# A chunked linear-attention and adapter kernel: 15 of 24 key products move from VectorE to GpSimd, gate selection moves to VectorE, and the written order is replaced

## The chip, the cores and the metric

The kernel runs on one core of a Trainium2 chip. The metric is device time in microseconds (us), from several executions of the whole kernel; lower is better. One execution was taken with the hardware profiler. Its page gives a span, from the first to the last instruction, and the run itself a slightly longer time.

The engines are TensorE (PE, with weight loads as PEld), VectorE (DVE), ScalarE (ACT), GpSimd (POOL) and SyncE (SP), which here only issues transfers. Each works through its own queue in order.

## The reference

Shapes are batch 4, 8 heads, 768 steps, head width 48. An attention with a decaying state is followed by a mixture of 8 adapters of rank 16, of which each row uses 2.

```python
for t in range(S):                                   # per batch and head
    cur = einsum('bhd,bhe->bhde', u[None] * kt, vt)
    y[:, :, t] = einsum('bhd,bhde->bhe', rt, state + cur)
    state = wt[:, :, :, None] * state + einsum('bhd,bhe->bhde', kt, vt)
...
x = y.transpose(0, 2, 1, 3).reshape(B * S, H * D)    # 3072 x 384
logits = x @ w_gate                                  # 8 adapters
topk = the 2 largest of each row;  w = exp(sel) / (sum + 1e-9)
out = x + sum over the 2 adapters e of  w * ((x @ A[e]) @ B[e])
```

## The kernel before

The rows are cut into 24 tiles of 128 steps. Tiles 0 to 5 are the chunks of the first batch, 6 to 11 of the second, and so on. Eight heads of 48 channels are kept as four pairs (`P` = 4), each pair on 128 partitions with the 48 channels of a head padded to 64. Logarithms of the decay are summed along a chunk by matrix products, so that within a tile the recurrence becomes two products with exponentials, a masked 128 x 128 score matrix per head, and a state that is carried from tile to tile.

The steps of one tile, by their names in the order string, with the engine that does them:

- `load_rk`, `load_w` (two tiles at once), `store`: transfers on SP's queue. `load_v`: a transfer on POOL's queue, which turns float32 into float16; `VGROUPS` says how many tiles each one brings. `rk_in` has 12 buffers, `w_in` 8, `res` 16.
- `ln` (ACT): logarithm of two tiles of decay. `cs` (PE): cumulative sums into the one buffer `cs_ps`. `expP`, `expN` (ACT): exponentials of the sum and of its negative, into `eP` and `eN`, one PSUM buffer each.
- `multR`, `multK` (DVE, lines 264 and 268): r times `eP` and k times `eN`, called `rseq` and `kT` in the profile.
- `kT` (PE, line 317): four transposes of the k product. `kev`: their copy to SBUF. `kv` (PE): the state's update in PSUM. `sev`: the state's copy to SBUF.
- `amm` (PE, line 305): scores. `aev` (DVE, line 311): scores times the mask. 
- `rku` (POOL, line 278): r times k, `dg` (PE): its sums with u, `dgev` (ACT): their copy for two tiles, `dv` (POOL, line 295): v times those sums.
- `yd`, `yA` (PE): the output y in PSUM. `yev`: its copy `xT`.
- `lg` (PE), `gate` (ACT, the exponential), `gmax` (DVE: largest values, sum, reciprocal), `gsel` (POOL, lines 393 to 396: which of the 8 values reach the second largest, times their weight), `z` (PE), `zw` (DVE), `zT` (PE), `zTev`: the adapters, in `BATCHES` of 4, 4, 4, 4, 4, 3 and 1 tiles; a step's number is that of the last tile of its batch.
- `d` (PE), `oev`: result and its copy `res`, which `store` writes out.

The order of all of this is written out by hand in the string `PLAN`, some 616 tokens such as `multK.7`. Walking through it issues each step's instructions, and every engine runs its own in that order. The copies go through one helper, which picks ACT or DVE; a star after a token swaps the two. The PSUM tiles `y_ps`, `kn_ps`, `z_ps`, `zT_ps`, `d_ps` and the warming `j_ps` come from one ring of two buffers. `setup` fills constants and runs `JUNK` warming matrix products.

```python
    for f, t, other in plan():
        side["other"] = other
        fns[f](t)
```

The functions that the change touches:

Of the kernel before, what the change touches and what calls it, by code (L numbers as in the profile page):

```python
# [8 lines left out]
F32 = mybir.dt.float32  # L9
# [12 lines left out]
VGROUPS = {0: 1, 1: 3, 4: 4, 8: 4, 12: 4, 16: 4, 20: 4}  # L22
JUNK = 8

PLAN = """
    setup.0 load_wa.0 load_w.2 load_wb.0 ln.0 cs.0 ln1.0 expN.0 expP.0 load_rk.0 load_rk.1 ln.2 junk.13 junk.3 cs.1
    multK.0 kT.0 multR.0 amm.0 kev.0 expN.1 junk.5 adapters.0 load_w.4 expP.1 multK.1 multR.1 cs.2 aev.0 casts.0*
    kT.1 load_rk.2 expN.2 multK.2 load_v.0 load_v.1 rku.1 junk.2 kv.0 expP.2 rku.0 dg.0 dg.1 cs.3 multR.2 load_rk.3
    amm.1 kev.1* dgev.1 ln.4 load_rk.4 sev.0 aev.1 load_w.6 dv.0 load_rk.5 yd.0 expP.3 load_rk.6 expN.3 kv.1
    load_v.4 sev.1 multR.3 yA.0 kT.2 multK.3 rku.2 cs.4 rku.3 yev.0 kev.2 amm.2 expP.4 dv.1 load_w.8 dg.2 rku.4 kT.3  # L30
    load_rk.7 expN.4 multR.4 dg.3 cs.5 multK.4 ln.6 yd.1 dgev.3 aev.2 rku.5 kv.2 dv.2 yA.1 expP.5 expN.5 dg.4
    multK.5 yev.1 kev.3* cs.6 multR.5 sev.2 dv.3 load_rk.8 amm.3 kT.4 dg.5 expN.6 kv.3 expP.6 yd.2 kev.4* rku.6 yA.2
    load_w.10 sev.3 cs.7 lg.1 aev.3 multK.6 yev.2 amm.4 yd.3 dgev.5 multR.6 dg.6 expN.7 expP.7 ln.8 yA.3 kT.6 kev.6*
    yev.3 load_w.12 aev.4 kv.4 lg.0 amm.5 dv.4 sev.4 multK.7 cs.8 multR.7 yd.4 kT.7 lg.2 rku.7 dg.7 expP.8 dv.5
    load_v.8 load_rk.9 lg.3 expN.8 adapterB.0 dgev.7 aev.5 kev.7* yA.4 multR.8 load_rk.10 amm.6 multK.8 kv.6
    load_rk.11 dv.6 rku.8 cs.9 yev.4 ln.10 gate.3 load_w.14 expP.9 expN.9 aev.6 yd.5 rku.9 yd.6 yA.5 amm.7 yev.5
    gmax.3 multR.9 yA.6 aev.7 multK.9 cs.10 yev.6 kT.8 gsel.3 z.3 sev.6 lg.5 dv.7 load_rk.13 ln.12 amm.8 kv.7 kev.8*
    kT.9 expP.10 zw.3 dg.9 dg.8 expN.10 yd.7 rku.10 load_rk.12 load_rk.14 dgev.9 kev.9* aev.8 load_rk.15 multR.10
    dv.8 load_w.16 yA.7 rku.11 sev.7 cs.11 zT.3 kv.8 multK.10 load_w.18 yev.7 zTev.3 dv.9 castB.0 dg.10 amm.9
    expP.11 sev.8* kT.10 d.0 kev.10 dg.11 load_v.12 expN.11 multR.11 rku.13 multK.11 cs.12 rku.12 ln.14 oev.0  # L40
    expP.12 d.1 oev.1 lg.4 expN.12 aev.9 yd.8 lg.7 kv.9 dgev.11 multR.12 yA.8 dv.10 yd.9 cs.13 amm.10 dv.11 sev.9
    yev.8 yA.9 expP.13 rku.14 multK.12 kv.10 d.2 dg.12 expN.13 aev.10 yev.9 rku.15 lg.6 cs.14 multR.13 gate.7 yd.10
    multK.13 oev.2 yA.10 store.0 sev.10 expP.14 amm.11 kT.12 dg.13 load_rk.16 lg.8 yev.10 expN.14 gmax.7 lg.9 kev.12
    kT.13 gsel.7 store.2 dgev.13 d.3 kev.13* oev.3 ln.16 aev.11 multR.14 cs.15 multK.14 z.7 kv.12 zw.7 expP.15 dv.13
    dv.12 ln.18 rku.16 amm.12 dg.14 kT.14 expN.15 dg.15 yd.11 yA.11 dgev.15 store.1 load_v.16 lg.10 load_rk.18 cs.16
    load_rk.17 kev.14* dv.15 yev.11 sev.12 zT.7 yd.12 aev.12 amm.13 yA.12 multR.15 store.3 rku.18 multK.15 expP.16
    zTev.7 expN.16 kv.13 aev.13 lg.11 multR.16 yev.12 dg.16 load_rk.19 gate.11 multK.16 d.7 oev.7 cs.17 d.4 sev.13
    yd.13 oev.4 gmax.11 amm.14 store.7 kv.14 yA.13 d.5 store.4 expP.17 expN.17 dv.14 aev.14 multR.17 yev.13 multK.17
    dg.18 lg.12 cs.18 kT.16 oev.5 rku.17 dg.17 kev.16* amm.15 kT.15 z.11 sev.14 kev.15* expP.18 yd.14 expN.18 yA.14
    aev.15 gsel.11 kv.15 zw.11 amm.16 rku.19 store.5 lg.13 load_w.20 load_rk.22 yev.14 zT.11 d.6 multK.18 cs.19  # L50
    dgev.17 zTev.11 sev.15 load_rk.21 oev.6 expN.19 d.9 yd.15 aev.16 store.6 oev.9 yA.15 amm.17 multR.18 aev.17
    dg.19 lg.14 d.8 yev.15 store.9 expP.19 oev.8 multR.19 dv.16 load_rk.20 ln.20 yd.16 lg.15 yA.16 kv.16 amm.18
    kT.18 load_rk.23 yev.16 gate.15 multK.19 kev.18 dv.17 rku.22 dgev.19 cs.20 sev.16 load_w.22 kT.19 gmax.15
    expP.20 store.8 load_v.20 kev.19 rku.21 d.10 oev.10 kv.18 dg.22 expN.20 dv.18 yd.17 sev.18 store.10 aev.18
    rku.20 yd.18 yA.17 yA.18 gsel.15 kv.19 amm.19 yev.17 yev.18 cs.21 dg.20 multK.20 kT.20 multR.20 aev.19 z.15
    expN.21 dv.19 lg.18 kev.20* multK.21 d.11 expP.21 dg.21 rku.23 amm.20 zw.15 lg.16 kT.21 ln.22 lg.17 oev.11 dg.23
    kev.21* sev.19 dgev.21 cs.22 zT.15 yd.19 yA.19 dgev.23 dv.20 expN.22 aev.20 multR.21 kv.20 zTev.15 multK.22
    yev.19 amm.21 d.12 yd.20 sev.20 dv.21 aev.21 oev.12 yA.20 yd.21 yA.21 kv.21 expP.22 lg.19 yev.20 d.13 multR.22
    yev.21 amm.22 sev.21 gate.19 dv.22 store.11 kT.22 cs.23 oev.13* d.15 kev.22* gmax.19 gsel.19 oev.15 store.12
    z.19 store.13 expP.23 yd.22 aev.22 zw.19 yA.22 kv.22 expN.23 multR.23 lg.21 yev.22 zT.19 d.14 zTev.19 sev.22  # L60
    multK.23 lg.20 lg.22 oev.14 d.16 gate.22 d.18 amm.23 gmax.22 oev.16 aev.23 oev.18 dv.23 d.17 store.15 gsel.22
    oev.17 z.22 zw.22 store.14 yd.23 yA.23 store.16 zT.22 yev.23 lg.23 zTev.22 d.21 d.19 gate.23 store.18 gmax.23
    oev.21 store.17 oev.19 d.22 z.23 oev.22 gsel.23 zw.23 store.21 zT.23 d.20 zTev.23 store.19 oev.20 d.23 store.22
    oev.23 store.20 junk.12 store.23
# [20 lines left out]
def kernel(  # L85
# [10 lines left out]
    NT, L = rk.shape[0], 128  # L96
# [42 lines left out]
    def load_rk(t):  # L139
        rk_in = io.tile([L, 2, P, NQ], F32, name="rk_in", bufs=12)  # L140
        nc.sync.dma_start(out=rk_in, in_=rk[t])
        st[t]["rk"] = rk_in
# [8 lines left out]
    w_sb = const.tile([128, P, ER + E + 2], F32, name="w_sb")  # L151
    w16 = const.tile([128, P, ER + E + 2], FP16, name="w16")
# [98 lines left out]

    def expN(t):
        nc.scalar.activation(out=eN, in_=cs_ps, func=ACT.Exp, scale=-1.0)  # L253

    def mult_half(t, q):
        c = t % NC
        if c == 0 and q == 0:
            r_ = wk.tile([128, P, NC * 128 + 1], BF16, name="rseq")
            nc.vector.memset(r_[:, :, 0:1], 0.0)
            for i in range(NC):  # L260
                st[t + i]["rseq"] = r_
        a = c * 128
        if q == 0:
            nc.vector.tensor_mul(st[t]["rseq"][:, :, a + 1:a + 129], st[t]["rk"][:, 0, :, 1:129], eP)  # L264
            st[t]["rT"] = st[t]["rseq"][:, :, a:a + 128]
        else:
            st[t]["kT"] = wk.tile([128, P, 128], BF16, name="kT", bufs=3)
            nc.vector.tensor_mul(st[t]["kT"], st[t]["rk"][:, 1, :, 1:129], eN)  # L268
# [7 lines left out]
    def rku(t):  # L276
        p_ = wk.tile([128, P, 128], FP16, name="rku", bufs=3)
        nc.gpsimd.tensor_mul(p_, st[t]["rk"][:, 0, :, 0:128], st[t]["rk"][:, 1, :, 1:129])  # L278
        st[t]["rku"] = p_
# [34 lines left out]
    def kT(t):  # L314
        kn_ps = ring([128, H, 64], BF16, "kn_ps")
        for p in range(P):
            nc.tensor.transpose(kn_ps[:, 2 * p:2 * p + 2].rearrange("s a d -> s (a d)"), st[t]["kT"][:, p, :], ident)  # L317
        st[t]["kn_ps"] = kn_ps
# [22 lines left out]
    def yd(t):  # L341
# [5 lines left out]
        if t % NC > 0:  # L347
            for p in range(P):
                nc.tensor.matmul(y_ps[:, p, :], lhsT=st[t - 1]["S"][:, p].rearrange("a g e -> a (g e)"),  # L349
                                 rhs=s_["rT"][:, p], start=False, stop=False, skip_group_check=True)  # L350
# [11 lines left out]
    def yev(t):  # L362
        xT = wk.tile([128, P, 128], FP16, name="xT", bufs=10)
        copy("ACT", xT, st[t]["y_ps"])
        st[t]["xT"] = xT

    def lg(t):
        for p in range(P):
            nc.tensor.matmul(lg_ps[:, t % NSLOT, :], lhsT=st[t]["xT"][:, p, :], rhs=w16[:, p, ER:ER + E],
# [9 lines left out]
    def gmax(t):  # L379
# [4 lines left out]
        for i in range(n):  # L384
            nc.vector.max(out=top[:, i, :], in_=ge[:, i, :])
        nc.vector.tensor_reduce(out=den, in_=top[:, :, 0:2], axis=AX.X, op=ALU.add)
# [3 lines left out]
    def gsel(t):  # L390
        t0, n = gate_at[t]
        g = wk.tile([L, GMAX, E], F32, name="g")[:, 0:n, :]
        nc.gpsimd.tensor_sub(g, st[t]["ge"], st[t]["top"][:, :, 1:2].to_broadcast([L, n, E]))
# [3 lines left out]
        st[t]["g"] = g  # L397

    def z(t):
        t0, n = gate_at[t]  # L400
        z_ps = ring([L, GMAX, ER], F32, "z_ps")
        for i in range(n):
            for p in range(P):
                nc.tensor.matmul(z_ps[:, i, :], lhsT=st[t0 + i]["xT"][:, p, :],
# [3 lines left out]
    def zw(t):  # L408
        t0, n = gate_at[t]
        zw_ = wk.tile([L, GMAX, E, R], FP16, name="zw")  # L410
        nc.vector.tensor_mul(
# [3 lines left out]
        st[t]["zw"] = zw_  # L415
# [95 lines left out]
```

## Time and profile before

| | |
|---|---|
| median of 3 runs | 93.3 us (92.87 to 94.39) |
| profiled execution, its own time | 94.24 us |
| its span | 92.5 us |
| busy: PE / DVE / ACT / POOL | 78.5 / 71.8 / 73.2 / 57.4 us |
| busy share of the DMA engines by the loads and stores on SP's queue | 66.2% of the span |
| the same by the v loads on POOL's queue | 14.3% |

In the rows of instruction groups "mean ns" is one instruction from start to end. Instructions of one engine overlap a little, so that counts times means come to more than the busy time: for DVE the groups add up to some 79 us against 71.8 busy, for ACT to some 88 against 73.2. Idle time stands with what ended it, inferred from semaphores. PE's busy time is modelled and a busy PE is not necessarily PE at its peak.

### The profile page before, as it was taken

Reading aid. Unit: us, or ns where it says so; the run is one execution under the profiler, and the core shown is the slowest. Engines: PE = TensorE matmul, PEld = TensorE weight load, DVE = VectorE, ACT = ScalarE, POOL = GpSimd, SP = SyncE. Lnnn points to the kernel's source line nnn. Section 1 sums busy time; section 2 is a strip of 40 time slices with the busy share of each in tenths; the row PEclk is TensorE's granted clock in tenths of the full one; section 3 lists DMA queues with packets and bytes.
Section 4 is the critical chain, followed back from the end, with each engine's and each line's share of the span. In section 5 each row is a group of like instructions: output and inputs, shape, how many; then the busy total and the mean of one; then the engine's idle time right before and its main releaser. Section 6 shows DMA issues by size and latency. Waiting matters only on the chain.

```text
span 92.5 us, 3554 instructions
## 1 busy us (share of the span) xinstructions
PE 78.5 (85%) x1430; PEld 61.2 (66%) x1430; DVE 71.8 (78%) x150; ACT 73.2 (79%) x163; POOL 57.4 (62%) x95
## 2 busy tenths in 40 slices
PE   2964855699899999799999999999959799998760
PEld 1323543585778888598888879887757578966420
DVE  5205918986989999998999999999499587987310
ACT  5219593988899999999999999899753997884640
POOL 6700939905996984999989984539378181612300
PEclk9999999957999999999999999999999999999999
DMA  1989999999999999999989997999995102418163
GB/s 34 262 296 328 283 409 416 378 292 403 416 417 401 394 284 377 413 360 257 311 227 352 293 215 223 348 355 327 278 250 155 64 32 92 170 43 301 46 252 137
DMA packets 10097, 25.19 MB, mean 272 GB/s; under 512 B 1120, under 2 KB 4704, under 8 KB 10080
## 3 DMA queue, kind: packets, MB, share of 16 engines
q1 hardware_dynamic: 9072, 22.60, 66.2%
q0 software_dynamic: 1008, 2.36, 14.3%
q8 instruction: 11, 0.18, 0.8%
q14 instruction: 6, 0.05, 0.2%
HBM read 22.60 MB, written 4.72 MB: 295 GB/s over the span
## 4 chain that ended last, share of the span: by engine, by line
DMA 43%; PE 22%; DVE 15%; POOL 6%; issue 4%; ACT 3%; SPq 3%; POOLq 0%; DVEq 0%
DMA rk_in<-in_rk_dram 21%; DMA w_in<-in_w_dram 10%; DMA v<-in_v_dram 9%; DVE at L311 7%; POOL rku L278 4%; DVE rseq L264 3%; PE y_ps L359 3%; PE y_ps L345 3%; PE d_ps L436 3%; POOL dv L295 2%; DVE kT L268 2%; PE y_ps L349 2%; DMA out_dram<-res 2%; PE a_ps L305 2%; PE d_ps L438 2%
## 5 line engine op out<-in xcount | busy, mean ns | idle before, releaser
L278 POOL TENSOR_TENSOR rku<-rk_in 128x512 f16<-128x512 f32 x24 | 25.9, 1087 | 11.9 <-DMA rk_in<-in_rk_dram 11.8
L311 DVE TENSOR_TENSOR at<-a_ps,at_mask 128x1024 f16<-128x1024 f32 x24 | 29.1, 1215 | 0.9 <-PE a_ps L305 0.7
L295 POOL TENSOR_TENSOR dv<-v,dg 128x384 f16<-128x384 f16 x24 | 19.6, 829 | 8.6 <-ACT dg L289 7.1
L268 DVE TENSOR_TENSOR kT<-rk_in,eN 128x512 bf16<-128x512 f32 x24 | 16.3, 680 | 10.5 <-DMA rk_in<-in_rk_dram 6.5
L120 ACT CAST xT<-y_ps 128x512 f16<-128x512 f32 x24 | 14.4, 608 | 3.1 <-PE y_ps L359 3.0
L264 DVE TENSOR_TENSOR rseq<-rk_in,eP 128x512 bf16<-128x512 f32 x24 | 16.3, 678 | 0.0
L250 ACT ACTIVATE eP<-cs_ps 128x512 f32<-128x512 f32 x24 | 14.5, 603 | 1.9 <-DVE rseq L264 1.4
L244 PE MATMUL cs_ps<-co_excl,logw 128*128 128x128 f16 x80 | 11.5, 223 | 4.1 <-ACT eP L250 2.5
L253 ACT ACTIVATE eN<-cs_ps 128x512 f32<-128x512 f32 x24 | 14.3, 596 | 0.7 <-DVE kT L268 0.6
L246 PE MATMUL cs_ps<-incl,logw 128*128 128x128 f16 x96 | 13.2, 226 | 0.6 <-ACT logw L226 0.6
L120 ACT COPY res<-d_ps 128x384 f32<-128x384 f32 x23 | 11.1, 488 | 1.8 <-PE d_ps L438 1.7
L246 PEld LDWEIGHTS <-logw 128*128 128x128 f16 x96 | 9.3, 101 | 4.3 <-issue 2.9
L226 ACT ACTIVATE logw<-w_in 128x768 f16<-128x768 f32 x11 | 9.5, 866 | 1.6 <-DMA w_in<-in_w_dram 1.6
L345 PE MATMUL y_ps<-ident,dv 128*128 128x128 f16 x96 | 9.6, 223 | 0.9 <-POOL dv L295 0.8
L305 PE MATMUL a_ps<-rseq,kT 48*128 48x128 bf16 x192 | 9.6, 218 | 0.2 <-DVE rseq L264 0.2
L359 PE MATMUL y_ps<-at,v 128*48 128x128 f16 x192 | 9.7, 226 | 0.0
L244 PEld LDWEIGHTS <-logw 128*128 128x128 f16 x80 | 7.7, 99 | 2.9 <-ACT eP L250 2.4
L120 ACT CAST S_sb<-s_ps 128x384 bf16<-128x384 f32 x19 | 9.5, 503 | 0.0
L436 PE MATMUL d_ps<-ident,xT 128*128 128x96 f16 x96 | 8.0, 205 | 0.4 <-ACT res L120 0.2
L349 PE MATMUL y_ps<-rseq,S_sb 128*128 128x128 bf16 x80 | 8.0, 224 | 0.0
L317 PE MATMUL kn_ps<-ident,kT 128*128 128x128 bf16 x80 | 7.8, 220 | 0.2
L438 PE MATMUL d_ps<-Ball,zT 128*128 128x384 f16 x24 | 7.8, 326 | 0.0
(68 smaller groups left out, 137.9 us busy)
## 6 DMA issues: line engine op xcount, KB each, us to landing
rk_in<-in_rk_dram SPq DMA_DIRECT2D x24, 516.0 KB, 9.8
out_dram<-res SPq DMA_DIRECT2D x24, 192.0 KB, 2.8
w_in<-in_w_dram SPq DMA_DIRECT2D x11, 384.0 KB, 10.9
v<-in_v_dram POOLq DMA_DIRECT2D x5, 384.0 KB, 8.5
w_in<-in_w_dram SPq DMA_DIRECT2D x2, 192.0 KB, 3.6
v<-in_v_dram POOLq DMA_DIRECT2D x1, 288.0 KB, 8.8
w_sb<-in_weights_dram SPq DMA_DIRECT2D x1, 276.0 KB, 7.8
B_sb<-in_moe_B_dram SPq DMA_DIRECT2D x1, 192.0 KB, 9.0
```

The source lines that it names most:

```text
L120: nc.scalar.copy(out=out, in_=in_)
L244: nc.tensor.matmul(cs_ps[:, p], lhsT=pair(st[t - 1]["logw"], p), rhs=co_excl, start=False, stop=False, skip_group_check=True)
L246: nc.tensor.matmul(cs_ps[:, p], lhsT=pair(st[t]["logw"], p), rhs=incl, start=False, stop=True, skip_group_check=True)
L250: nc.scalar.activation(out=eP, in_=cs_ps, func=ACT.Exp)
L253: nc.scalar.activation(out=eN, in_=cs_ps, func=ACT.Exp, scale=-1.0)
L264: nc.vector.tensor_mul(st[t]["rseq"][:, :, a + 1:a + 129], st[t]["rk"][:, 0, :, 1:129], eP)
L268: nc.vector.tensor_mul(st[t]["kT"], st[t]["rk"][:, 1, :, 1:129], eN)
L278: nc.gpsimd.tensor_mul(p_, st[t]["rk"][:, 0, :, 0:128], st[t]["rk"][:, 1, :, 1:129])
L295: nc.gpsimd.tensor_mul(dv_[:, :, 0:D], st[t]["v16"], st[t]["dg"].rearrange("p (h o) -> p h o", o=1).to_broadcast([L, H, D]))
L311: nc.vector.tensor_mul(at, st[t]["a_ps"].rearrange("s g p f -> s (g p) f"), at_mask.to_broadcast([128, H, 128]))
L345: nc.tensor.matmul(y_ps[:, p, :], lhsT=pair(s_["dv"], p), rhs=ident16, start=(p == 0), stop=False, skip_group_check=True)
L359: nc.tensor.matmul(y_ps[b:b + D, p, :], lhsT=s_["v16"][:, 2 * p + g], rhs=s_["at"][:, g * P + p], start=False, stop=True, skip_group_check ...
```

## The change

- Fifteen `multK` steps carry a star (tiles 0, 2, 3, 5, 8, 9, 11, 13, 14, 16, 17, 19, 21, 22, 23) and run on POOL. For these, `expN` writes its exponential to SBUF, into one of two buffers `eN_sb`; the other nine keep DVE and `eN` in PSUM.
- `gsel` for the six batches of 3 or 4 tiles runs on DVE, as one compare-and-multiply for each tile and one product for the batch. The batch of one tile (tile 23) folds selection and weight into `gmax` and `zw`.
- `kT` transposes 112 rows into 112 columns instead of 128 into 128.
- `VGROUPS` splits tiles 1 to 3 into groups of 1 and 2, so there are 8 loads of v and not 7. `JUNK` goes from 8 to 4. `xT` has 14 buffers instead of 10.
- `LK` is the partition count of the input `rk`, which is 128 as before, so every slice `[0:LK]` is the whole tile.
- `PLAN` is new throughout. Of the copies, `kev` is on DVE for 12 tiles and on ACT for 8 (before: 6 and 14), `sev` on DVE for 4 (before: 1), `yev` for 1 (before: 0), `oev` for 2 (before: 1), `zTev` on ACT for 2 batches (before: 0), and the two casts of weights are on DVE (before: ACT).
- In the new order the transfers on SP's queue begin wa, wb, rk.0, adapters, rk.1, w.2, rk.2, w.4, rk.3, w.6, rk.4, rk.5, rk.6; before they began wa, w.2, wb, rk.0, rk.1, adapters, w.4, rk.2, rk.3, rk.4, w.6, rk.5, rk.6. Two stores (3 and 4) stand ahead of the load of w.22 and four (3, 4, 1, 0) ahead of the last load, rk.23; before, nine stood ahead of rk.23 and w.22, the last two.

```diff
-VGROUPS = {0: 1, 1: 3, 4: 4, 8: 4, 12: 4, 16: 4, 20: 4}
-JUNK = 8
+RKBUFS = 12
+VGROUPS = {0: 1, 1: 1, 2: 2, 4: 4, 8: 4, 12: 4, 16: 4, 20: 4}
+JUNK = 4
...
-    setup.0 load_wa.0 load_w.2 load_wb.0 ln.0 cs.0 ln1.0 expN.0 expP.0 load_rk.0 load_rk.1 ln.2 junk.13 junk.3 cs.1
-    multK.0 kT.0 multR.0 amm.0 kev.0 expN.1 junk.5 adapters.0 load_w.4 expP.1 multK.1 multR.1 cs.2 aev.0 casts.0*
...
+    setup.0 load_wa.0 load_wb.0 load_rk.0 adapters.0 ln.0 load_v.0 load_rk.1 junk.3 ln1.0 casts.0 load_w.2 cs.0
+    junk.8 load_rk.2 expP.0 multR.0 junk.1 expN.0 multK.0* load_v.1 cs.1 kT.0 amm.0 expP.1 rku.0 expN.1 rku.1 kev.0
...
+    k_on_pool = {t for f, t, other in plan() if f == "multK" and other}
+
     def expN(t):
-        nc.scalar.activation(out=eN, in_=cs_ps, func=ACT.Exp, scale=-1.0)
+        st[t]["eN"] = wk.tile([128, P, 128], F32, name="eN_sb") if t in k_on_pool else eN
+        nc.scalar.activation(out=st[t]["eN"], in_=cs_ps, func=ACT.Exp, scale=-1.0)
...
-            st[t]["kT"] = wk.tile([128, P, 128], BF16, name="kT", bufs=3)
-            nc.vector.tensor_mul(st[t]["kT"], st[t]["rk"][:, 1, :, 1:129], eN)
+            st[t]["kT"] = wk.tile([LK, P, 128], BF16, name="kT", bufs=3)
+            eng = nc.gpsimd if t in k_on_pool else nc.vector
+            eng.tensor_mul(st[t]["kT"], st[t]["rk"][:, 1, :, 1:129], st[t]["eN"][0:LK])
...
-            nc.tensor.transpose(kn_ps[:, 2 * p:2 * p + 2].rearrange("s a d -> s (a d)"), st[t]["kT"][:, p, :], ident)
+            nc.tensor.transpose(kn_ps[:, 2 * p:2 * p + 2].rearrange("s a d -> s (a d)")[:, 0:64 + D],
+                                st[t]["kT"][0:64 + D, p, :], ident[0:64 + D, 0:64 + D])
...
-        xT = wk.tile([128, P, 128], FP16, name="xT", bufs=10)
+        xT = wk.tile([128, P, 128], FP16, name="xT", bufs=14)
...
+        if n == 1:
+            g = wk.tile([L, GMAX, E], F32, name="g")[:, 0:n, :]
+            nc.vector.tensor_add(den[:, 0], top[:, 0, 0:1], top[:, 0, 1:2])
+            nc.vector.scalar_tensor_tensor(out=g[:, 0], in0=ge[:, 0], scalar=top[:, 0, 1:2], in1=ge[:, 0],
+                                           op0=ALU.is_ge, op1=ALU.mult)
+            nc.vector.reciprocal(out=den[:, 0], in_=den[:, 0])
...
+        if side["other"]:
+            for i in range(n):
+                nc.vector.scalar_tensor_tensor(out=g[:, i], in0=st[t]["ge"][:, i], scalar=st[t]["top"][:, i, 1:2],
+                                               in1=st[t]["ge"][:, i], op0=ALU.is_ge, op1=ALU.mult)
+            nc.vector.tensor_mul(g, g, st[t]["den"].to_broadcast([L, n, E]))
+            return
...
+        if n == 1:
+            nc.vector.scalar_tensor_tensor(
+                out=zw_[:, 0], in0=st[t]["z_ps"][:, 0].rearrange("p (e r) -> p e r", r=R), scalar=st[t]["den"][:, 0],
+                in1=st[t]["g"].rearrange("p n (e o) -> p (n e) o", o=1).to_broadcast([L, E, R]),
+                op0=ALU.mult, op1=ALU.mult)
```

## The prediction

> **What bounds the kernel now.** I read the page's busy times and slices first, then busy time by stretches, because the stages have different limits, then waits, the chain that ended last, and groups by shape.
>
> ```profile
> PE 78.5 (85%) x1430; PEld 61.2 (66%) x1430; DVE 71.8 (78%) x150; ACT 73.2 (79%) x163; POOL 57.4 (62%) x95
> PEclk9999999957999999999999999999999999999999
> DMA  1989999999999999999989997999995102418163
> ```
>
> ```profile
> core 0: us, PE busy (x) PEld busy (x) DVE busy (x) ACT busy (x) POOL busy (x), PEclk, DMA share, GB/s
> 0.00:8.00 8.00, 4.55 (x16) 1.79 (x16) 1.90 (x15) 3.24 (x6) 3.31 (x14) 1.00 0.68 218
> 8.00:25.00 17.00, 13.13 (x207) 9.63 (x208) 13.45 (x22) 13.39 (x29) 10.67 (x12) 0.90 1.05 366
> 25.00:45.00 20.00, 19.45 (x411) 16.23 (x408) 19.22 (x36) 19.76 (x47) 17.35 (x23) 1.00 1.03 360
> 45.00:65.00 20.00, 20.00 (x421) 17.12 (x420) 19.73 (x45) 19.34 (x47) 15.60 (x25) 1.00 0.92 293
> 65.00:76.00 11.00, 9.11 (x183) 7.44 (x181) 8.44 (x11) 7.87 (x19) 6.71 (x11) 1.00 0.58 160
> ```
>
> There are four stages. Until 25 us DMA is full and DVE and ACT idle 3.6 us of 17: the inputs set the pace. From 25 to 65 us DVE (38.95 of 40), ACT (39.10) and PE are all full and POOL has 7 us spare. From 65 to 76 us all have holes. Then comes the tail of dependent steps.
>
> The holes are a late input, by the waits and the chain (start, length, what):
>
> ```profile
> POOL rku L278 <- DMA rk_in<-in_rk_dram: 11.8, 4, 5.3
> POOL dv L295 <- ACT dg L289: 7.1, 4, 2.5
> ACT logw L226 <- DMA w_in<-in_w_dram: 1.6, 1, 1.6
> ...
> SPq L447 <- ACT res L120: 31.7, 15, 7.4
> ```
>
> ```profile
> 62.08 9.48 DMA w_in<-in_w_dram
> 71.56 0.02 issue
> 71.59 0.85 ACT logw L226
> ```
>
> SP's queue holds loads behind stores, and a store waits for its result. So w.22 is issued only at 62.08 and lands at 71.56, and tiles 22 and 23 start from there.
>
> **What the Trainium skill says.** (1) "GPSIMD Engine Reference", 3.1, puts an elementwise product at about twice DVE's time. Here the same shape with both inputs in SBUF takes 1.087 us on POOL (rku) against 0.680 on DVE (kT), 1.6 times. (2) "ScalarE: Activation LUTs", "Step-by-step: what each stage is for", calls PSUM the faster destination for ScalarE. Here it hardly shows: eN to PSUM takes 596 ns, xT of the same size to SBUF 608. I take 0.01 us for each exp moved. (3) "SBUF — State Buffer", "Who interferes with whom", says that a DVE instruction with two SBUF inputs contends with a GpSimd instruction that reads SBUF, and that one fully blocks until the other ends. The new gate selection has two SBUF inputs; no large DVE step before has. The trace of before has only a weak hint against it: a DVE cast from SBUF to SBUF, a form that the page also lists as a contender, ran inside a POOL instruction.
>
> ```profile
> 2.60 0.34 POOL masks.py:66 TENSOR_SCALAR_AFFINE_SELECT at_mask<-at_mask 128x128 f16<-128x128 f16 x1
> 2.65 0.13 DVE L208 CAST ident<-ident 128x128 f16<-128x128 bf16 x1
> ```
>
> **The change part by part.** Prices are group means:
>
> ```profile
> L278 POOL TENSOR_TENSOR rku<-rk_in 128x512 f16<-128x512 f32 x24 | 25.9, 1087 | 11.9 <-DMA rk_in<-in_rk_dram 11.8
> L268 DVE TENSOR_TENSOR kT<-rk_in,eN 128x512 bf16<-128x512 f32 x24 | 16.3, 680 | 10.5 <-DMA rk_in<-in_rk_dram 6.5 <-ACT S_sb L120 2.3 <-ACT xT L120 1.3
> L120 ACT COPY kn<-kn_ps 128x384 bf16<-128x384 bf16 x14 | 6.9, 492 | 1.0 <-PE kn_ps L317 0.7 <-PE s_ps L283 0.2
> L122 DVE COPY kn<-kn_ps 128x384 bf16<-128x384 bf16 x6 | 2.0, 341 | 0.0
> L385 DVE MAX8 top<-ge 128x8 f32<-128x8 f32 x24 | 2.3, 153 | 0.9 <-ACT ge L376 0.9
> ```
>
> DVE: 15 K products leave, -15 x 0.680 = -10.2. Arriving: 6 kev x 0.341 = 2.05; 3 sev x 0.544 = 1.63; one yev 0.68 (zw's row, same size); one oev 0.56; the two casts about 1.1 (0.65 from ACT's row, and 0.45, between kn and res); less 2 zTev x 0.418 = -0.84. Gate selection is 23 compare-multiplies at MAX8's 0.153 = 3.5 and 6 products at about 0.2 (reciprocal 0.178) = 1.2; the last batch adds 0.15. The sum is -0.2: **DVE is not relieved.** What leaves is filled up from ACT and POOL.
>
> ACT: -6 x 0.492 - 3 x 0.503 - 0.608 - 0.488 - 0.652 - 0.597 + 2 x 0.6 = -5.6; times busy over summed time (73.2 / 88) that is -4.7.
>
> POOL: +15 x 1.087 = 16.3; seven selections leave, about -6.9 (four instructions of 0.24 to 0.29 each); one more v load, +0.6. So +10, to 67.4. It fills the room of the full stage (7 of 40 us) nearly up.
>
> PE: the chain has four transposes at 0.33 us. At 112 of 128 columns they save 0 to 0.04 a tile, at most 0.8 over 20 tiles; I take 0.3. Four warming products fewer lie before PE has work; the clock already falls to 0.5 and 0.7 in slices 9 and 10, where PE is not the limit, so nothing, at worst 0.5. Four more xT buffers cost nothing, and `LK` is 128, so those slices change nothing.
>
> Start: ahead of and including rk.0 SP now issues 192 + 192 + 516 = 900 KB, before 192 + 384 + 192 + 516 = 1284. The 384 KB less are 1.2 us at the 321 GB/s of 5 to 10 us. Tile 0 starts that much earlier, but by rk.6 both orders have issued the same set, and until 25 us DMA is full. So tile 4's scores, at 25.69 before, gain little. I take 0.5, between 0 (the K products of tiles 0, 2, 3 and 5 queue on POOL, whose rku and dv wait behind them) and 1.2.
>
> Middle: the same DVE work on a full DVE is worth nothing. ACT's 4.7 us end only the waits for ACT; DVE's short ones from 25 to 76 us, and PE's, are some 1 us. I take half, 0.5.
>
> Loads: only stores 3 and 4 stand ahead of w.22 now, and stores 1 and 0, whose results are early, ahead of rk.23. By counts of ACT work ahead of it, store 4 has its result where the fourth to sixth did before, near 46 us. So the last load is issued near 48, not 62. From the issue rows I add all loads to 20.2 MB, with four stores 21.0. Of these 15.2 are moved by 45 us at the old rates, and the other 5.8 take 16 us at 360 GB/s or 20 at 293: last landing at 61 to 65 us, not 71.56. That removes DVE's holes of 65 to 76 us, 2.56, but for some remainder: I take 2.3, between 1.0 and 2.6. Next late is DVE itself.
>
> Tail: for tile 23 the selection of four POOL instructions goes. From the largest value (86.31) to zw (87.72) is 1.41 us; maximum, sum, compare and reciprocal on DVE come to some 0.65. Gain 0.75.
>
> Added waits: a K product on POOL takes 0.41 longer, and behind it wait that tile's transposes and scores on PE, then aev on DVE, and rku and dv in its own queue. The two eN buffers free ACT from waiting for it. Where the order leaves half a microsecond it is hidden. I take 0.5 in all, 0 to 6 (the rival below). Gate selection against POOL's reads: 0.2, from 0 to one POOL instruction for each of five instructions, 5.2 a batch.
>
> Sum: -0.5 - 0.5 - 2.3 - 0.75 - 0.3 + 0.5 + 0.2 = -3.65. The profiled execution took 94.24 (span 92.5 and 1.74 around it), so about 90.6. The median is 0.94 lower, so **89.7 us**, a gain of 3.9%.
>
> **Rivals.** A, slower: POOL becomes the bound. After tile 4's scores, near 25 us, it has 67.4 less some 20 = 47 us of work, about 45 when overlapped, and its last K product is due before aev.23, which the forecast puts near 80 us: some 54 us of room, so 8 to 9 us of slack. Before, it idled 7.1 us for dg alone. If waits at the head of its in-order queue pass 8.5 us, each further one delays K products and so PE, DVE and everything. Twice the old ones, 14 us and more, would add about 6: 96. For: four queues at 90% and over, each in order. Against: most rk waits are before 25 us, and selections, which made POOL wait for DVE, are gone. B, slower: the shared SBUF interface. With POOL nearly always busy in the five batches up to tile 19, a wait of one POOL instruction a batch costs 5 x 1.04 = 5.2, which turns the gain into a loss of 1.5; two waits give 100. For: the page; against: the cast above. C, no change: the loads come early, but DVE, PE and ACT at 97% leave no room, and POOL's new waits of 2 to 3 us eat the gain: 92.5. Also, the change might not do what it says; here it does, but moving work off DVE is undone by what moves onto it.
>
> **How the numbers follow.** Forecast 0.56 (its own range 86.8 to 91.4: start, loads and transposes at their best, or half the gain). C 0.19, A 0.15, B 0.10. Faster by over 2% means below 91.4, slower above 95.2; about 2% is what a measurement of this kernel can tell from no change. So 0.56, 0.19, 0.25. For 8 times in 10 the range leaves out the far part of A and B: 86.8 to 96.5.
>
> **What would show it.** Right: DVE busy within 1.5 of 71.8, ACT near 68.5, POOL near 67; the last rk or w landing before 66 us; no wait of ACT for w_in late; aev.23 started near 80 us, not 83.08; DVE full from 25 us until then. Wrong: long waits of PE or DVE for POOL's kT or dv (A); compare-multiplies that start about 1 us apart (B); last loads still landing near 71 us, or DVE idle as much as before at 65 to 76.

## The result, and the profile after

The changed kernel takes **108.84 us** (median, 108.01 to 109.22) against 93.09 for the kernel before beside it: a ratio of 1.170 with a 95% interval of 1.159 to 1.182. The forecast was 89.7 with a range up to 96.5, so sign and size are wrong. The profiled execution took 109.17, its span 107.5. Here and below a ratio compares undisturbed executions alone and so can differ from the quotient of two medians, and decides where it does; where too few executions were undisturbed, none is given.

Busy times and slices of the page, changed kernel:

```profile
PE 85.8 (80%) x1426; PEld 67.7 (63%) x1426; DVE 84.8 (79%) x176; ACT 70.6 (66%) x152; POOL 68.6 (64%) x83
PEclk9998558999589955799965699999999859999996
DMA  3999999999999995002999999869340025014463
```

Busy time by stretches:

```profile
core 0: us, PE busy (x) PEld busy (x) DVE busy (x) ACT busy (x) POOL busy (x), PEclk, DMA share, GB/s
25.00:45.00 20.00, 16.78 (x271) 13.83 (x271) 17.13 (x30) 13.55 (x31) 15.74 (x17) 0.74 0.87 305
45.00:65.00 20.00, 16.30 (x289) 13.95 (x288) 16.92 (x36) 13.55 (x31) 11.96 (x14) 0.83 0.73 243
```

POOL (67.4 forecast) is near its sum, and ACT (68.5) 2 us above it. DVE is 13 us over its 71.6. The full stage of before, 25 to 65 us, is gone: no engine is full in it, PE's granted clock falls to 0.74 and 0.83, and DMA stands still near 45 us. The groups of instructions say where DVE's 13 us are (the last two columns are mean ns and idle time before):

```profile
L412 DVE SCALAR_TENSOR_TENSOR g<-ge,top 128x8 f32<-128x8 f32 x23 | 15.5, 733 | 0.0
L273 POOL TENSOR_TENSOR kT<-rk_in,eN_sb 128x512 bf16<-128x512 f32 x15 | 17.7, 1179 | 10.7 <-PE s_ps L375 4.9
```

The compare-multiplies of the gate selection were priced at 153 ns, MAX8's duration. They take 733 on the mean, with no idle time ahead: their wait is inside the instruction, so it shows as busy time, and no view of waits names it. The instruction's own list (shortest, median, longest ns) shows how far they spread:

```profile
L412 DVE SCALAR_TENSOR_TENSOR g<-ge,top x23: 198/465/3568, 32.4 to 98.9; 128x8 f32<-128x8 f32 x23
```

One by one, ten of the 23 take 0.20 to 0.26 us, two 0.39 and 0.47, ten between 0.82 and 1.21, and one 3.57. The timelines of both engines show what they wait for. First the batch with the longest, DVE and then POOL (start, length, what):

```profile
31.75 0.68 DVE L268 TENSOR_TENSOR rseq<-rk_in,eP 128x512 bf16<-128x512 f32 x1
32.35 3.98 DVE L412 SCALAR_TENSOR_TENSOR g<-ge,top 128x8 f32<-128x8 f32 x4
36.36 0.19 DVE L414 TENSOR_TENSOR g<-g,den 128x32 f32<-128x32 f32 x1
```

```profile
30.80 2.12 POOL L283 TENSOR_TENSOR rku<-rk_in 128x512 f16<-128x512 f32 x2
32.89 0.82 POOL L300 TENSOR_TENSOR dv<-v,dg 128x384 f16<-128x384 f16 x1
33.68 1.08 POOL L283 TENSOR_TENSOR rku<-rk_in 128x512 f16<-128x512 f32 x1
34.72 1.17 POOL L273 TENSOR_TENSOR kT<-rk_in,eN_sb 128x512 bf16<-128x512 f32 x1
35.84 0.59 POOL L148 DMA_DIRECT2D v<-in_v_dram  x1
```

Of the four, one lasts 3.57 us and three about 0.21. The long one ends when POOL's last product ends and POOL only issues a transfer. So it did not wait for the one POOL instruction alone that ran when it began, but through four products that followed one another without a gap.

The other four batches beside POOL look different. The fourth, DVE's compare-multiplies and then POOL's products one by one:

```profile
80.39 0.47 DVE L412 SCALAR_TENSOR_TENSOR g<-ge,top 128x8 f32<-128x8 f32 x1
80.78 1.12 DVE L412 SCALAR_TENSOR_TENSOR g<-ge,top 128x8 f32<-128x8 f32 x1
81.82 1.12 DVE L412 SCALAR_TENSOR_TENSOR g<-ge,top 128x8 f32<-128x8 f32 x1
82.87 0.21 DVE L412 SCALAR_TENSOR_TENSOR g<-ge,top 128x8 f32<-128x8 f32 x1
```

```profile
79.74 1.09 POOL L283 TENSOR_TENSOR rku<-rk_in 128x512 f16<-128x512 f32 x1
80.78 1.09 POOL L283 TENSOR_TENSOR rku<-rk_in 128x512 f16<-128x512 f32 x1
81.83 1.09 POOL L283 TENSOR_TENSOR rku<-rk_in 128x512 f16<-128x512 f32 x1
```

Here each of the first three waits for one product, the one that runs beside it, and ends 0.02 to 0.03 us after it. The next compare-multiply then meets the next product, though these products too follow one another without a gap. So it is in the second, third and fifth batch as well: in the four batches 12 compare-multiplies waited in this way. Why one instruction in the first batch waited through four products is not shown. The last batch of three, with POOL idle, is the control:

```profile
98.67 0.47 DVE L412 SCALAR_TENSOR_TENSOR g<-ge,top 128x8 f32<-128x8 f32 x3
```

At the control's 0.47 us for three, 23 are 3.6 us of busy time; 15.5 were measured: 11.9 us of hidden waiting, 3.4 in the first batch and 1.0 to 2.9 in each of the other four. Behind a stopped DVE the other engines stop too. In the chain that ended last line 412 alone holds 14%, and store 3 with the loads behind it stands on SP's queue until 49.61 us. The waits (total, times, longest) have PE idle behind zw, and ACT behind PE:

```profile
PE kn_ps L322 <- DVE zw L440: 4.8, 2, 3.7
...
ACT eP L251 <- PE a_ps L310: 3.7, 1, 3.7
```

### The profile page after: what moved, and what is told of

Read it like the earlier page. It is cut to its first block, busy times and chain, and to the rows that moved or that the text cites. A ratio compares the mean times of both kernels' runs of the same rounds, so it can differ in the third digit from the quotient of the medians.

```text
span 107.5 us, 3533 instructions
## 1 busy us (share of the span) xinstructions
PE 85.8 (80%) x1426; PEld 67.7 (63%) x1426; DVE 84.8 (79%) x176; ACT 70.6 (66%) x152; POOL 68.6 (64%) x83
## 4 chain that ended last, share of the span: by engine, by line
PE 35%; DVE 32%; DMA 19%; issue 5%; ACT 4%; SPq 2%; DVEq 0%; ACTq 0%
DMA w_in<-in_w_dram 19%; DVE g L412 14%; DVE at L316 6%; DVE zw L440 4%; PE d_ps L464 4%; PE a_ps L310 4%; PE y_ps L365 3%; PE cs_ps L247 3%; PE y_ps L351 3%; PE cs_ps L245 3%; DVE rseq L268 3%; PE kn_ps L322 3%; PE y_ps L355 3%; PE d_ps L466 2%; PE zT_ps L449 2%
## 5 line engine op out<-in xcount | busy, mean ns | idle before, releaser
L273 POOL TENSOR_TENSOR kT<-rk_in,eN_sb 128x512 bf16<-128x512 f32 x15 | 17.7, 1179 | 10.7 <-PE s_ps L375 4.9
L268 DVE TENSOR_TENSOR rseq<-rk_in,eP 128x512 bf16<-128x512 f32 x24 | 16.3, 679 | 2.4 <-ACT eP L251 1.4
L247 PE MATMUL cs_ps<-incl,logw 128*128 128x128 f16 x96 | 15.6, 251 | 0.0
L412 DVE SCALAR_TENSOR_TENSOR g<-ge,top 128x8 f32<-128x8 f32 x23 | 15.5, 733 | 0.0
L245 PE MATMUL cs_ps<-co_excl,logw 128*128 128x128 f16 x80 | 13.5, 248 | 1.1 <-ACT eP L251 0.6
L310 PE MATMUL a_ps<-rseq,kT 48*128 48x128 bf16 x192 | 11.1, 243 | 3.0 <-DVE at L316 2.4
L322 PE MATMUL kn_ps<-ident,kT 112*128 112x112 bf16 x80 | 8.5, 238 | 6.1 <-DVE zw L440 4.8
L247 PEld LDWEIGHTS <-logw 128*128 128x128 f16 x96 | 10.6, 114 | 3.0 <-issue 2.2
L257 ACT ACTIVATE eN_sb<-cs_ps 128x512 f32<-128x512 f32 x15 | 9.1, 608 | 2.9 <-PE cs_ps L247 2.6
L322 PEld LDWEIGHTS <-kT 112*128 112x128 bf16 x80 | 5.7, 109 | 7.2 <-issue 5.6
L310 PEld LDWEIGHTS <-kT 48*128 48x128 bf16 x192 | 6.5, 103 | 6.0 <-issue 4.4
L245 PEld LDWEIGHTS <-logw 128*128 128x128 f16 x80 | 8.9, 113 | 1.4 <-ACT eN_sb L257 1.2
```

The source lines that it names most:

```text
L245: nc.tensor.matmul(cs_ps[:, p], lhsT=pair(st[t - 1]["logw"], p), rhs=co_excl, start=False, stop=False, skip_group_check=True)
L247: nc.tensor.matmul(cs_ps[:, p], lhsT=pair(st[t]["logw"], p), rhs=incl, start=False, stop=True, skip_group_check=True)
L273: eng.tensor_mul(st[t]["kT"], st[t]["rk"][:, 1, :, 1:129], st[t]["eN"][0:LK])
L310: nc.tensor.matmul(a_ps[:, g, p, :], lhsT=k_[b:b + D, p, :], rhs=rT[b:b + D, p, :], start=True, stop=True, skip_group_check=True)
L412: nc.vector.scalar_tensor_tensor(out=g[:, i], in0=st[t]["ge"][:, i], scalar=st[t]["top"][:, i, 1:2], in1=st[t]["ge"][:, i], op0=ALU.is_ge, ...
```

## The experiments

Medians in us. "Before" in the same session ran at 92.4 to 93.9.

| run | what | median | ratio to before, 95% interval |
|---|---|---|---|
| e1 | changed kernel, selection back on POOL | 105.44 | 1.128 (1.117 to 1.139) |
| e2 | changed kernel, selection compares logits in PSUM | 98.22 | 1.030 (1.016 to 1.044) |
| e3 | before, selection on DVE | 101.46 | |
| e4 | before, 15 K products on POOL | 108.62 | 1.164 (1.150 to 1.177) |
| e7 | e4 with the first v loads first | 105.26 | 1.147 (1.134 to 1.160) |
| e5 | changed kernel, stores late | 107.95 | 1.177 (1.158 to 1.196) |
| e6 | e2, stores late | 100.38 | 1.092 (1.078 to 1.107) |
| e8 | new order alone | 103.48 | 1.126 (1.115 to 1.138) |
| e9 | changed kernel, no selection in the six large batches | 89.41 | 0.975 (0.964 to 0.986) |
| e10 | before, no selection | 92.76 | 1.014 (1.006 to 1.022) |
| e15 | new order, K on DVE, no selection | 100.24 | 1.096 (1.083 to 1.110) |
| e13 | changed kernel, compare with one SBUF input | 95.72 | 1.045 (1.035 to 1.056) |
| e16 | the same, reciprocal first | 99.81 | 1.073 (1.062 to 1.083) |
| e17 | e16, stores late | 100.07 | |
| e18 | e16, one cast back on ACT | 93.86 | 1.021 (1.011 to 1.031) |
| e11 | before, stores late | 91.07 | 0.986 (0.981 to 0.991) |
| e12 | e11 and three small parts | 91.33 | 0.992 (0.987 to 0.997) |
| e14 | e11, K of tiles 20 to 23 on POOL | 93.53 | 1.022 (1.013 to 1.031) |

### First cut: the selection, in both orders

e1 puts the six selections back on POOL, e2 keeps them on DVE but gives the compare one operand from PSUM, e3 moves them to DVE in the kernel before.

```diff
 e1
-        if side["other"]:
+        if False:
 e2  (per tile; topl = the largest logits, den folded into zw tile by tile)
-  scalar_tensor_tensor(out=g[:, i], in0=ge[:, i],    scalar=top[:, i, 1:2],  in1=ge[:, i])
-  tensor_mul(g, g, den)
+  scalar_tensor_tensor(out=g[:, i], in0=lg_ps[...],  scalar=topl[:, i, 1:2], in1=ge[:, i])
```

> The changed kernel with the gate selection of the six larger batches put back on POOL, nothing else. Theory (a selection on DVE reads two SBUF inputs and waits until POOL's run of instructions has a gap): the 15.5 us of compare-multiplies leave DVE, some 12 of them waiting, POOL gets about 6 us more; the time falls from 108.8 to 94-99 us. Rival (POOL has become the bound by its K products): POOL gets still more work, so the time stays at 105 us or rises.

> The changed kernel with the selection still on DVE, as many compare-multiplies as before at the same places in the order, but comparing the logits where they lie in PSUM with their own maximum, so that only one input is in SBUF (four more maxima a batch, the weight folded into zw by one instruction a tile; the result is the same). Theory: mean compare-multiply falls from 733 ns to 150-250, whatever POOL does, and the time to 94-98 us; below 94 if all the rest of the change is worth something. Rival (POOL as the bound, or DVE simply having too many small instructions): 105 us or more, the small instructions being as many.

> The kernel before with the selection alone moved to DVE (all batches of 3 or 4). Theory: POOL runs without a gap in the full stage here too, so compare-multiplies take 0.4-0.8 us on the mean and the time rises by 3-9 us, to 96-102. Rival (only the new K products on POOL make it slow): within 2% of 93.

e1 took 105.44, where 94 to 99 was expected: DVE falls to 72.0 busy, but POOL rises to 74.2, and DVE's zw waits 8.7 us for POOL's g. That is the rival's number, but not its reason alone: from 25 to 65 us POOL is busy for only 31 of 40 us and waits 5.6 us for PE, and a cast on DVE loses some 4 us (below). e2 took 98.22 (96.11 to 101.33) though it adds 23 maxima and a slower zw: its compare-multiplies take 218 ns on the mean. e3 costs some 8%; there, with POOL 51.7 busy, they take 285 ns, less than was expected, and only some 2 of the 6.4 us that DVE works longer are waiting. That the rest costs time because DVE was full is read from this, not tried.

### K products on POOL alone, in the old order

```diff
 e4
+    k_on_pool = {0, 2, 3, 5, 8, 9, 11, 13, 14, 16, 17, 19, 21, 22, 23}
+            eng = nc.gpsimd if t in k_on_pool else nc.vector
 e7  (also)
-    setup.0 load_wa.0 ... multK.2 load_v.0 load_v.1 rku.1
+    setup.0 load_v.0 load_v.1 load_wa.0 ... multK.2 rku.1
```

> The kernel before with the same 15 K products moved to POOL alone (eN in SBUF for them), order unchanged. Theory (selection did the harm): between 90 and 96 us, as DVE loses 9 us and POOL gains 16. Rival A (POOL's queue as the bound): 100 us or more.

> The kernel before with 15 K products on POOL, and the loads of v for tiles 0 to 3 issued first on POOL's queue. With K products alone moved (108.6 us) the v loads stood behind the first of them and PE waited 8.3 us for v. Theory (that wait was the start's part, POOL's queue the rest): 98-103 us. Rival (K products on POOL do no harm by themselves): 91-95.

e4 took 108.62 and e7 105.26, though DVE falls to 64.5. In e4 the v loads stand behind the first K product on POOL's queue, and PE waits 8.3 us for v; e7 removes that. POOL is then busy for 37.5 of 40 us between 25 and 65, PE waits 6.9 us for POOL's rku (its weight loads 8.2), and from 8 to 25 us DVE works 8.21 of 17 us. e4 came out as its rival had it, e7 above both of its expectations. So an in-order POOL is the bound when K products are added and nothing is re-ordered: rival A is real too, in this order.

### Stores, and the order alone

e5 and e6 put the stores 3, 4, 1 and 0 of the changed kernel and of e2 behind the last load. e8 is the changed kernel's order with all K products on DVE (seven of them issued earlier, so that the one `eN` buffer is free in time), selections on POOL and stores late.

```diff
 e5, e6, e8
-    ... oev.3 gmax.7 aev.11 expP.14 yd.10 store.3 amm.12 ... load_rk.23
+    ... oev.3 gmax.7 aev.11 expP.14 yd.10 amm.12 ... load_rk.23 store.3 store.4 store.1 store.0
```

> The changed kernel with stores 3, 4, 1 and 0 moved on SP's queue behind the last load, nothing else. In the changed kernel SP stood at store 3 until 49.6 us and DMA was idle before that. Theory (two separate causes: selection waits of some 12 us and this hole in the loads): DMA's hole goes, w.18 and the rk behind it land by 50 us, the time falls by 1-5 us, to 104-108. Rival (the hole costs nothing, since DVE stands in the selection meanwhile): within 1 us of 108.8.

> The changed kernel with the selection against the logits in PSUM and the four stores behind the last load. Without the selection waits the hole in the loads is the longest stall left (POOL idle 5.6 us, PE 3.9 us). Theory: 98.2 falls by 4-6, to 92-94. Rival (POOL's K products bound it): within 2 us of 98.2. If it is below 91 the rest of the change is worth what was forecast.

> The changed kernel's order with all K products on DVE (seven of them moved ahead of the exponential that would overwrite their input in the one PSUM buffer) and all selections on POOL, stores behind the last load. Theory (the order is planned for K on POOL): DVE gets 9 us more than in the changed kernel without waits, 95-99 us. Rival (the order by itself is better than the one before): below 92.

e5 took 107.95: the hole in DMA near 45 us goes, and the time stays within 1 us, as the rival had it. The hole was a result of DVE's stop, not a cause. e6 took 100.38, no gain either and above both expectations; by the ratios it is slower than e2 (1.092 against 1.030). e8 took 103.48, above its 95 to 99: the order by itself, with its division of the copies, is no gain. Beside e1, which differs from it by the K products on POOL and by early stores, it is level (1.126 and 1.128).

### The selection left out

```diff
 e9, e10, e15
     def gsel(t):
+        st[t]["g"] = st[t]["ge"]
+        return
```

> The changed kernel with the selection of the six large batches left out: zw takes all eight weights, no compare-multiply and no product with the reciprocal; the last batch of one tile keeps its selection. It shows what the rest of the change is worth when selection costs nothing. Theory 1 (the compare-multiplies' waits for POOL's gaps were the whole loss): 15.5 + 1.5 us of DVE work and waits leave and the time falls to 90 to 92.5 us, below the kernel before, with DVE near 68 busy. Theory 2 (POOL, with 15 K products in its in-order queue, and the new order hold the other engines up besides): 94 to 97, with holes of 2 us and more on PE and DVE behind POOL's kT, rku or dv.

> The kernel before with the selection of all seven batches left out (zw takes all eight weights): the partner of the changed kernel without selection. POOL loses 28 instructions, about 6.9 us, and nothing else changes. If POOL has slack before the change (7 of 40 us idle in the full stage, as the prediction read it): 92 to 93, no more than 1 us less than before, most of it in the tail. If POOL's queue is already near the limit: 88 to 90.

> The new order with all 24 K products on DVE (as in e8_order_only, seven of them moved ahead in the order and the four stores late), and with the selection of the six large batches left out, as in e9_after_no_selection. Beside that run (89.4) it tells what the K products on POOL are worth in the order that was made for them. If POOL's K products are what gains: DVE has 15 x 0.68 = 10.2 us more, 78 of busy time, and the time is 96 to 100. If the order alone (start, loads, tail) gains: 89 to 92.

These kernels let all eight adapters in where the choice of two is left out: in the six large batches in e9 and e15, in all seven in e10. Without it the kernel before gains nothing (92.76 against 92.91), and the changed one falls from 108.84 to 89.41, a little below its expectation. Its full stage is full again, POOL included:

```profile
25.00:45.00 20.00, 19.85 (x417) 16.26 (x414) 18.55 (x37) 19.17 (x46) 19.36 (x22) 1.00 0.96 331
45.00:65.00 20.00, 19.40 (x414) 16.10 (x411) 18.46 (x40) 18.43 (x42) 19.06 (x21) 1.00 1.03 356
```

So 19.4 us by the medians, some 18 by the ratios, hang on the selection; DVE's busy time falls by 16.3 of them (84.8 to 68.5). e15, with the K products back on DVE (seven of them earlier, and the stores late, which e5 showed to be worth nothing), takes 100.24: in the order written for it and without selection, K on POOL is worth 10.8 us, where it cost 13 in the old order (e7). With the selections on POOL as well it was worth nothing in the new order either (e1 beside e8), though e1 also bears the cast's wait.

### Wait or work: one operand in PSUM, then one cast

e13 keeps number and shape of the selection's DVE instructions. ScalarE writes the exponential a second time, in place over the logits in PSUM, and the compare reads it there.

```diff
 e13
+            nc.scalar.activation(out=lg_ps[:, q:q + n, :], in_=lg_ps[:, q:q + n, :], func=ACT.Exp)
-  scalar_tensor_tensor(out=g[:, i], in0=ge[:, i],   ..., in1=ge[:, i])
-  tensor_mul(g, g, den)
+  scalar_tensor_tensor(out=lg_ps[i], in0=lg_ps[i],  ..., in1=ge[:, i])
+  tensor_mul(g, lg_ps[...], den)
 e16
+  tensor_mul(gd, lg_ps[...], den)
+  scalar_tensor_tensor(out=g[:, i], in0=lg_ps[i],   ..., in1=gd[:, i])
```

> The changed kernel with the same number and shapes of selection instructions on DVE (23 compare-multiplies, 5 products), but each reads one tensor from PSUM and one from SBUF: ScalarE writes the exponential of a batch a second time, in place over the logits in PSUM (six more small ScalarE instructions, about 1.5 us in all), and the compare-multiply reads that and overwrites it. If the waits for POOL come from the two SBUF inputs, the mean of a compare-multiply falls from 733 ns to 160 to 230, DVE to 73 to 75 busy and the time to 91 to 95: the kernel without selection (89.4) plus about 5 us of selection on a DVE that is full to nine tenths. If DVE waits for POOL for another reason (the place of the selections in the order), they stay at 700 ns and the time above 104.

95.72, so 13.1 us come back (the ratio falls from 1.170 to 1.045). The instruction's list, to be held against that of line 412:

```profile
L415 DVE SCALAR_TENSOR_TENSOR s_ps<-s_ps,top,ge x23: 222/234/235, 31.2 to 85.8; 128x8 f32<-128x8 f32 x23
```

The longest is 235 ns, not 3568, in the same places of the order, with POOL's products running beside them and POOL as busy (68.5). That settles it: the wait is tied to both inputs lying in SBUF. That e13 also writes its result to PSUM is not the reason: e2 and e16 write to SBUF and take no more than 227 ns. The time is just above the 91 to 95 that was expected.

> As e13_gsel_one_sbuf_input, but the reciprocal is multiplied in first (one product for a batch from PSUM), and the compare-multiplies write to SBUF, so that DVE no longer writes into the PSUM tile s_ps, which the state's accumulation and its copy share. In e13 the selection waited 3.5 us, most of it for matrix products and copies on that tile. If these waits were made by the writes: 1.5 to 3 us less, 92.5 to 94. If the reads alone make them: 95 to 96.5, as e13.

> The run above with the four stores behind load_rk.23. In the changed kernel and in its PSUM-sided version this was worth nothing, since other waits were later. If the late w loads (w.18 and what stands behind store 3) are now among the last to arrive: 1 to 2 us less than the run above, as in the kernel before (1.3). If not: within 0.7 us of it.

99.81 and 100.07: e16 is slower than e13, against both of its expectations, with compare-multiplies of 220 ns, and late stores again change nothing. e16's DVE and POOL timelines show a second victim:

```profile
35.68 4.80 DVE L123 CAST Ball<-B_sb 128x384 f16<-128x384 f32 x1
40.40 0.34 DVE L123 COPY kn<-kn_ps 128x384 bf16<-128x384 bf16 x1
```

```profile
34.81 0.59 POOL L148 DMA_DIRECT2D v<-in_v_dram  x1
35.42 0.84 POOL L300 TENSOR_TENSOR dv<-v,dg 128x384 f16<-128x384 f16 x1
36.22 1.08 POOL L283 TENSOR_TENSOR rku<-rk_in 128x512 f16<-128x512 f32 x1
37.26 0.82 POOL L300 TENSOR_TENSOR dv<-v,dg 128x384 f16<-128x384 f16 x1
38.05 1.08 POOL L283 TENSOR_TENSOR rku<-rk_in 128x512 f16<-128x512 f32 x1
39.09 1.16 POOL L273 TENSOR_TENSOR kT<-rk_in,eN_sb 128x512 bf16<-128x512 f32 x1
```

The cast of moe_B, which the change moved from ACT to DVE, has one input, in SBUF, and its output in SBUF. It starts 0.26 us after the first of five products without a gap and ends 0.23 after the last. In e9 it starts inside POOL's DMA issue instead and takes 0.35:

```profile
35.11 0.35 DVE L123 CAST Ball<-B_sb 128x384 f16<-128x384 f32 x1
```

```profile
34.62 0.59 POOL L148 DMA_DIRECT2D v<-in_v_dram  x1
35.24 0.91 POOL L300 TENSOR_TENSOR dv<-v,dg 128x384 f16<-128x384 f16 x1
```

In the changed kernel it starts just ahead of a product and takes as little, and there the product takes longer, 1.29 us instead of 1.08:

```profile
40.79 0.35 DVE L123 CAST Ball<-B_sb 128x384 f16<-128x384 f32 x1
```

```profile
40.80 1.29 POOL L283 TENSOR_TENSOR rku<-rk_in 128x512 f16<-128x512 f32 x1
```

e18 changes one token of e16, the cast's engine.

```diff
-    ... aev.8 expN.12 castB.0* dv.8 kev.9
+    ... aev.8 expN.12 castB.0 dv.8 kev.9
```

> As e16_gsel_den_first, with one token changed: the cast of moe_B (Ball, 128x384, from SBUF to SBUF) is on ScalarE, as in the kernel before. In e16 this cast began at 35.68 us, 0.26 after POOL's dv, and ended at 40.48, 0.2 after the last of five POOL instructions without a gap: 4.80 us instead of 0.35 where it began inside POOL's DMA issue (35.11 us, in the version without selection). If a DVE cast with its input and output in SBUF waits for POOL's gap as the compare-multiplies do, and all behind it: 4 to 6 us less than e16, 93.5 to 96, and the 6.2 us that POOL waits for s_ps and PE's 4.0 for kn go. If the cast's length has another cause or the time is lost elsewhere anyway: 98 to 100.

93.86: 5.9 us by the medians and 5.2% by the ratios from one token, at the good end of the expectation. The cast also took 4.78 us in the profile of e17, 4.49 in those of e2 and e6 and 4.15 in that of e1; in the changed kernel itself, e5 and e13 it took 0.35 to 0.38. That it made e2 and e6 slow is read from their traces and not tried apart. From the changed kernel to e18 it is 15.0 us (the ratio falls from 1.170 to 1.021), and DVE's busy time falls from 84.8 to 72.3.

### Smaller parts of the change, in the old order

```diff
 e11
-    ... load_rk.16 ... store.2 ... load_rk.23 ... load_w.22
+    ... load_rk.16 ... load_rk.23 ... load_w.22 store.0 store.2 store.1 store.3 store.7 store.4 store.5 store.6 store.9
 e12  (also: 112-wide transposes, xT bufs=14, the last batch folded into gmax and zw)
 e14  (e11, also)
+    k_on_pool = {20, 21, 22, 23}
```

> The kernel before with its nine stores ahead of the load of w.22 put behind it, all else as before. It tries the prediction's step 'Loads' in the place where it was read. Theory 1 (the step is right: DVE's holes of 65 to 76 us, 2.56, are waits for rk and w behind stores): w.22 lands before 66 us and the time falls by 1.0 to 2.6 us, to 90.7 to 92.3. Theory 2 (the load is early but the full engines or the buffers of rk_in take over, as with the stores in the changed kernel): within 0.7 us of before.

> The kernel before with stores late as in the run above, and with three more parts of the change that put nothing on a full engine: transposes 112 wide, 14 xT buffers, and selection and weight of the last batch of one tile folded into gmax and zw on DVE, when POOL has nothing else to do. K products and the other six selections stay where they were. By the prediction's steps it gains 2.3 + 0.3 + 0.75 = 3.35: about 90 us. If the loads' step is worth nothing, only the tail and the transposes count: 92 to 92.5.

> The kernel before with stores late (91.1), and the K products of the last four tiles, 20 to 23, on POOL from an exponential in SBUF; all else as in that run. From 65 us on POOL has 11 us idle there and DVE is full (10.2 of 11). If moving a K product pays where POOL has room: DVE loses 4 x 0.68 = 2.7 us, of which 1 to 2 come out at the end: 89 to 90. If a K product on POOL costs its reader more than it saves DVE (1.18 us against 0.68, and behind rku and dv in the queue): 91 to 93.

e11, 91.07, is 1.4% faster than the kernel before, a small gain but clear of the noise, and as expected. The load of w.22 is issued at 46.10 us, not 62.08, and from 65 to 76 us DVE works 10.19 and not 8.44:

```profile
65.00:76.00 11.00, 11.00 (x237) 9.46 (x235) 10.19 (x20) 9.77 (x23) 6.05 (x12) 1.00 0.28 89
```

e12 (91.33) adds nothing to it, where about 90 was expected. Its zw of the last tile is released by PE's z, not by the selection:

```profile
84.19 0.35 DVE L423 SCALAR_TENSOR_TENSOR zw<-z_ps,den,g 128x128 f16<-128x128 f32 x1 [0.77 <-PE z_ps L414]
```

e14 goes from 1.4% faster to 2.2% slower, worse than either expectation, although POOL had room there (6.05 of 11 us busy). Now POOL is busy for 9.58 of these 11 us and DVE for only 7.82; PE waits 0.7 us for POOL's kT, and behind it ACT's kev 0.6 and DVE's aev 1.1. At this place too, K products added to POOL's queue delayed more than they relieved.

## Why the prediction was wrong, point by point

- **"Gate selection against POOL's reads: 0.2" is the step that failed.** It measured some 12 us on DVE (11.9 by the durations; 84.8 against 72.3 busy in e18, which has one cast of 0.4 less) and 15.0 in time. The mechanism was right and was named, as rival B at 10%. "SBUF — State Buffer", "Who interferes with whom", in the Trainium skill says that a DVE instruction with two SBUF inputs, or a cast in one of DVE's fast modes, contends with GpSimd; e13 agrees for the two inputs, and the cast of 4.80 us in e16 fits, though no run shows in which mode it ran. The step was set aside for one cast that ran beside a POOL instruction at 2.65 us, which was a mask setup and no product: not the same case, and why it was not held up is not shown. And rival B priced one wait a batch, 5.2 us in all, where in four of the five batches each compare-multiply that met POOL waited for a product of its own: 1.0 to 3.4 us in each of the five. That lies inside the step's own range, up to 5.2 a batch; the 0.2 taken from this range rested on that cast alone. With 11.9 in place of 0.2 the sum would have given 101.4, so by this estimate the engines behind DVE lost another 7 us on the way to 108.8.
- **What shows it**, "compare-multiplies that start about 1 us apart (B)", came true: 80.78, 81.82 and 82.87 in the fourth batch, and much the same in the second and fifth. Only the first batch, with one instruction of 3.57 us and three short ones, was not foreseen.
- **The DVE sum** held: 72.3 in e18 against 71.6. **The two casts**, priced at 1.1 us of work, hid up to 4.4 us of waiting in one of them (4.80 against 0.35). In the changed kernel it cost DVE no wait by luck: it started 0.01 us ahead of a POOL product.
- **"K product on POOL added waits 0.5, 0 to 6"**: in the new order without selection the K products gain 10.8 us (e9 against e15), with the selections on POOL nothing (e1 against e8); in the old order they cost 13 to 15. A price for the move without its order and its neighbours on POOL has no meaning. The duration was 1.18 us, not 1.087.
- **Loads (2.3, between 1.0 and 2.6)** were right as a mechanism: e11 gains 1.4%, 1.3 us, in the place from which the step was read; aev.23 starts at 80.34 there. In the changed kernel store 4's result was to come near 46 us; store 3, ahead of it, waits until 49.61, because DVE had stopped. Moving the stores out of the way there gains nothing (e5).
- **Start (0.5)** was too low: DVE takes up tile 4's scores at 23.55 us and not 25.69, 2.1 earlier, more than the range allowed, and e9 keeps a lead (22.75).
- **Tail (0.75) and transposes (0.3)** are not found: e12 is not faster than e11. From the largest value of tile 23 to zw it takes 1.33 us, 1.41 in e11, since PE's z is next late.
- **ACT** came to 70.6, not 68.5; nothing was seen to hang on it. **Rival A** was real for e4 and e7, in part perhaps for e1, not for the changed kernel.
- Without selection (e9) the gain is 3.5 us by the medians and 2.5% by the ratio, near the forecast's 3.65, but that is luck and not its proof: the forecast was for a kernel with some 5 us of selection work on DVE, which e9 leaves out. With the work and without the waits (e18) the kernel is 2.1% slower than before by the ratio, so a second part of the forecast failed that the 0.2 does not cover. **Open** is how much of the 4.5 us from e9 to e18 is the work itself and how much is in e18's own edit, whose selection waits 2.7 us for matrix products and copies on the PSUM tile that it reads.

## What to carry to other kernels

Before an instruction is moved to DVE beside a busy GpSimd, look at where its inputs lie. With two in SBUF, or as a cast from SBUF to SBUF, price each such instruction, however small, at one GpSimd product, and at worst at a whole run of products without a gap, with everything queued behind it; with one of two inputs in PSUM it ran at its own length. In a trace such a wait is busy time: compare the durations of one shape with its shortest. A move between engines is worth what its order makes of it, so try the parts one at a time and also all but one.

## What the runs showed of the hardware

- A 128x8 compare-multiply with both inputs in SBUF took 0.20 us alone and up to 3.57 beside POOL; with one in PSUM never more than 0.24. POOL's products beside it kept their length (rku 1.07 to 1.10 us, 1.09 on the mean before), so it is DVE that waits.
- A waiting compare-multiply ended 0.02 to 0.03 us after a POOL product: 12 of them after the product that ran beside them, one only after four in a row. The cast of e16 ended only after five. What decides between the two is not shown.
- It is not always DVE that waits. The cast that started just ahead of a product took 0.35 us, and the product 1.29 instead of 1.08; in e13 it was 0.38 and 1.22.
- DVE's instructions with one of two inputs in PSUM (r times `eP`, 0.68 us before and after) and MAX8, with one input in SBUF (0.15 to 0.17 us), kept their length beside POOL in the changed kernel.
- PE's granted clock was 0.74 from 25 to 45 us in the changed kernel, where PE stood for up to 3.7 us behind zw, and 1.00 in e9 in the same stretch, where it was busy for 19.85 of 20 us. No run tries how much of the lost time is the clock's.
